# A 128-byte pad among the constants of a fused attention and two-layer feed-forward kernel

## The chip, the cores and the metric

The kernel runs on one core of one Trainium2 chip. A core has five engines that run side by side: TensorE (PE, with its weight loads shown as PEld), VectorE (DVE), ScalarE (ACT), GpSimd (POOL) and SyncE (SP, which only issues transfers here). They work on SBUF, which has 128 partitions, and on PSUM, where matmuls leave their sums. The metric is the device time of one execution in microseconds (us). Before the change the median of two runs is 689.15 us (688.72 and 689.59).

## The reference

Three stages follow each other. Everything is float32, and the weights of the two feed-forward layers come as float64.

```
kv  = einsum('bhsd,bhse->bhde', k, v)            # 4 x 8 heads, 576 tokens, 64 wide, no softmax
out = einsum('bhsd,bhde->bhse', q, kv)
out = out / sqrt(mean(out*out) + 1e-6) * g_norm  # per token and head
x   = out as [2304 tokens, 512]
x   = (x @ w_a) * (x @ w_b) @ w_out              # 512 -> 1536 -> 512
h   = x @ w_in                                   # 512 -> 1024
s   = h * softmax(h)
y   = (s - mean(s)) / sqrt(var(s) + 1e-6) * g_ln
return y @ moe2_w_out                            # 1024 -> 512
```

## The kernel before, in words

The kernel keeps float32 accuracy by splitting operands into a high and a low part in the format fp32r and adding three matmuls for each product (high by high, high by low, low by high; `three` at lines 763 to 767, and the loop at line 850).

**Attention** (lines 602 to 755). Per batch, `pkv` is k-transposed times v (L602, L609), copied to the block-diagonal tiles `bd` (L615). Per tile of 128 tokens, `o` is q times `bd` (L647); it is squared and summed, the root is taken on POOL (L677, with the constant `mhalf`), and the scaled tile is turned by a matmul against the constant `ident` (L742), then split into `xh` and `xl` (L754, L755). Later tiles are turned through DRAM instead.

**First layer**. Weights arrive as float64 bits (`raw`), and are decoded into high and low float32 parts by ACT, DVE and POOL (lines 333 to 354, 435 to 437), into the ring of tiles `wh`/`wl`. `ab` (L765 to L767) takes `wh`/`wl` as the stationary operand and `xh`/`xl` as the moving one; `y` (L850) takes `wh`/`wl` as stationary and `gh`/`gl` as moving, and DVE adds its result to `ya` (L863).

**Second layer**. `h` (L1013) is made with a scheme of seven products of half-size blocks, from `late` tiles (left) and `wd` or `late` tiles (left); `out` (L765 to L767 by way of `run_o`) takes `dh` (right) or a piece of a `late` tile (left) as stationary and `wh_o`/`wl_o` (right) or a piece of a `late` tile (left) as moving.

**What sets the order.** A planner, `Order`, runs while the program is written: it keeps a clock and a table of costs for each engine, and decides from them which matmul group, vector operation or transfer is written next. Its costs know nothing of addresses. On the chip every engine then runs its own list in that order, and semaphores hold it back where data is missing. All transfers are issued by SP.

**Where buffers lie.** SBUF is given out from both ends. The pools `cst` (constants), `xs` (`xh`, `xl`, later the `late` tiles), `att` (`bd`, `kv`, `tail`, `q`, `qs`, `x`, `sq`, `r`) and, in the place of `att`, `w2` (`wd`, `bt`) are opened with side="left". The pools `wp` (`wh`, `wl`), `yp` (`ya`), `ph1` (`raw`, `u`, `f`, `a`, `gh`, `gl`) and, in the place of `ph1`, `ph2` (`st`, `u`, `ot`, `dh`) with side="right". The change stands among the first lines that take tiles, 192 to 201:

```
    ident = cst.tile([P, P], F32, tag="ident", name="ident")
    ...
    mhalf = cst.tile([P, H], F32, tag="mhalf", name="mhalf")

    nc.gpsimd.memset(mhalf, -0.5)
    ...
    make_identity(nc, ident)
```

Of the kernel before, what the change touches and what calls it, by code (L numbers as in the profile page):

```python
# [9 lines left out]
F32 = mybir.dt.float32  # L10
# [7 lines left out]
P = 128  # L18
# [128 lines left out]
def attention_moe_moe_kernel(ctx: ExitStack, tc, kv_in, kv_tail, q_in, g_norm, w1, w_in, w_out2, g_ln, out):  # L147
# [3 lines left out]
    nc = tc.nc  # L151
    INF = float("inf")

    cst = ctx.enter_context(tc.tile_pool(name="cst", bufs=1, side="left"))
# [38 lines left out]
    gn = cst.tile([P, 1], F32, tag="gn", name="gn")  # L193
    gl_sb = cst.tile([P, NF2], F32, tag="gln", name="gln")
    mhalf = cst.tile([P, H], F32, tag="mhalf", name="mhalf")

    nc.gpsimd.memset(mhalf, -0.5)
    bds = [att.tile([P, NP, P], F32, tag=f"bd{n}", name=f"bd{n}", bufs=1) for n in range(2)]
# [1192 lines left out]
```

## Time and profile before

| | |
|---|---|
| median of two runs | 689.15 us (688.72 to 689.59) |
| the profiled execution | 688.91 us |
| its span, first to last instruction | 687.1 us |
| PE busy | 672.2 us (98%) |
| DVE, ACT, POOL busy | 522.9, 277.0, 274.6 us |
| granted TensorE clock, mean | 0.999 |

The profile is of one execution. Its span is 1.8 us shorter than that execution's time, and 2.05 us shorter than the median of the runs. A PE that is 98% busy says that some matmul was under way nearly always; how closely matmuls follow each other is read from their start times. Buffer numbers are left out of names, so `wh_w` stands for every high part of a first-layer weight.

### The profile page before, as it was taken

The page shows a single profiled execution, that of the slowest core. Times are in us where ns is not written, and L with a number is a line of the kernel's source. Part 1 is how long each engine was busy: PE and PEld are TensorE (multiplying, and loading weights), DVE is VectorE, ACT ScalarE, POOL GpSimd, SP SyncE. Part 2 cuts the span into 40 slices and gives each one's busy share as a digit, 9 for nine tenths or more (in the row PEclk, how much of TensorE's full clock was granted, in tenths as well). Part 3 has the DMA queues.
Part 4 walks back from the last instruction along what each step waited for, and adds up shares of the span by engine and source line. Part 5 has one row for each costly group of instructions (what it writes and reads, how often), then busy time and mean ns, then how long its engine had stood idle before and what let it go on. Part 6 is the DMA issues. An engine that isn't in the chain of part 4 may idle for free.

```text
span 687.1 us, 9551 instructions
## 1 busy us (share of the span) xinstructions
PE 672.2 (98%) x3530; PEld 582.8 (85%) x3530; DVE 522.9 (76%) x754; ACT 277.0 (40%) x481; POOL 274.6 (40%) x276
## 2 busy tenths in 40 slices
PE   5899999999999999999999999999999999999998
PEld 4799888989888898989898988889778888888887
DVE  2988875689989899889789798555559878766850
ACT  3768244423332333332233232211257665653531
POOL 1848213244374534633332232301448656651100
PEclk9999999999999999999999999999999999999999
DMA  8974340123242221123141422013422654354451
GB/s 328 374 269 134 106 139 1 62 96 119 92 154 93 79 74 62 62 93 124 61 154 65 133 80 93 0 62 114 174 80 83 193 155 129 103 151 139 152 170 47
DMA packets 63694, 82.42 MB, mean 120 GB/s; under 512 B 6176, under 2 KB 45344, under 8 KB 63648
## 3 DMA queue, kind: packets, MB, share of 16 engines
q1 hardware_dynamic: 63648, 81.81, 36.2%
q8 instruction: 28, 0.46, 0.3%
q14 instruction: 18, 0.15, 0.1%
HBM read 59.25 MB, written 22.54 MB: 119 GB/s over the span
## 4 chain that ended last, share of the span: by engine, by line
PE 93%; DMA 3%; SPq 1%; ACT 1%; DVE 1%; POOL 1%; issue 0%; ACTq 0%
PE y L850 21%; PE ab L765 14%; PE ab L767 14%; PE ab L766 14%; PE h L1013 13%; PE out L766 5%; PE out L767 5%; PE out L765 5%; PE o L647 1%; DMA kv<-in_kv 1%; DMA raw_w<-in_w 1%; DMA q<-in_q 1%; POOL r L677 1%; SPq L276 1%; PE pkv L602 0%; PE t L742 0%
## 5 line engine op out<-in xcount | busy, mean ns | idle before, releaser
L765 PE MATMUL ab<-xh,wh_w 128*128 128x512 f32 (+1 forms) x480 | 178.1, 371 | 0.0
L766 PE MATMUL ab<-xl,wh_w 128*128 128x512 f32 (+1 forms) x480 | 176.9, 369 | 0.2 <-DVE xl L755 0.2
L767 PE MATMUL ab<-xh,wl_w 128*128 128x512 f32 (+1 forms) x480 | 177.0, 369 | 0.0
L863 DVE TENSOR_TENSOR ya<-y,ya 128x1024 f32<-128x1024 f32 (+1 forms) x110 | 122.3, 1111 | 4.1 <-PE y L850 3.9
L819 ACT COPY a<-ab 128x512 f32<-128x512 f32 (+1 forms) x60 | 32.6, 544 | 204.5 <-PE ab L767 204.4
L436 POOL TENSOR_TENSOR f_w<-f_w,wh_w 128x512 f32<-128x512 f32 x36 | 48.3, 1343 | 157.1 <-ACT wh_w L435 87.2
L765 PEld LDWEIGHTS ab<-xh,wh_w 128*128 128x128 f32 x480 | 90.2, 188 | 12.9 <-DVE ya L863 1.0
L766 PEld LDWEIGHTS ab<-xl,wh_w 128*128 128x128 f32 x480 | 90.2, 188 | 12.0 <-DVE xl L755 0.5
L767 PEld LDWEIGHTS ab<-xh,wl_w 128*128 128x128 f32 x480 | 90.1, 188 | 11.3
L820 DVE TENSOR_TENSOR ab<-ab,a 128x512 f32<-128x512 f32 (+1 forms) x60 | 38.7, 644 | 72.1 <-ACT a L819 72.0
L850 PE MATMUL y<-gl,wh_w 128*128 128x512 f32 (+1 forms) x240 | 88.5, 369 | 0.3 <-DVE gl L822 0.3
L850 PE MATMUL y<-gh,wl_w 128*128 128x512 f32 (+1 forms) x240 | 88.5, 369 | 0.0
L850 PE MATMUL y<-gh,wh_w 128*128 128x512 f32 (+1 forms) x240 | 88.4, 368 | 0.0
L1013 PE MATMUL h<-wd,lateh 128*128 128x512 f32 x216 | 58.5, 390 | 0.7 <-ACT bt L1050 0.7
L943 POOL TENSOR_TENSOR lateh<-ya,lateh 128x512 fp32r<-128x512 f32 (+1 forms) x18 | 21.1, 1189 | 74.0 <-ACT lateh L942 74.0
L850 PEld LDWEIGHTS y<-gl,wh_w 128*128 128x128 f32 x240 | 45.0, 188 | 6.6 <-DVE gl L822 0.8
L437 POOL TENSOR_TENSOR wl_w<-f_w,u_w 128x512 fp32r<-128x512 f32 x36 | 47.7, 1328 | 6.0 <-DVE u_w L354 4.3
L850 PEld LDWEIGHTS y<-gh,wh_w 128*128 128x128 f32 x240 | 45.1, 188 | 5.8
L850 PEld LDWEIGHTS y<-gh,wl_w 128*128 128x128 f32 x240 | 45.1, 188 | 5.6
L1013 PEld LDWEIGHTS h<-wd,lateh 128*128 128x128 f32 x216 | 40.4, 188 | 9.5 <-ACT bt L1050 1.2
L821 ACT CAST gh<-ab 128x512 fp32r<-128x512 f32 (+1 forms) x60 | 32.7, 545 | 33.7 <-DVE ab L820 32.5
L1013 PE MATMUL h<-latel,lateh 128*128 128x512 f32 x162 | 45.7, 390 | 0.0
(114 smaller groups left out, 1164.6 us busy)
## 6 DMA issues: line engine op xcount, KB each, us to landing
raw_w<-in_w SPq DMA_DIRECT2D x36, 512.0 KB, 3.3
su<-ya SPq DMA_DIRECT2D x34, 256.0 KB, 2.9
ya<-su SPq DMA_DIRECT2D x34, 256.0 KB, 3.0
kv<-in_kv SPq DMA_DIRECT2D x16, 512.0 KB, 7.5
out<-ot SPq DMA_DIRECT2D x17, 256.0 KB, 3.2
raw_i<-in_w_in SPq DMA_DIRECT2D x8, 512.0 KB, 3.4
raw_o<-in_w_out SPq DMA_DIRECT2D x8, 512.0 KB, 3.7
so<-raw_o SPq DMA_DIRECT2D x8, 512.0 KB, 2.7
```

The lines of the kernel that those rows point to most:

```text
L436: ("T", 1.32, lambda: nc.gpsimd.tensor_tensor(out=f, in0=f, in1=hi.bitcast(F32), op=ALU.subtract)),
L437: ("T", 1.38, lambda: nc.gpsimd.tensor_tensor(out=lo, in0=f, in1=u, op=ALU.add)),
L765: nc.tensor.matmul(o, lhsT=ah, rhs=bh, start=first, stop=False)
L766: nc.tensor.matmul(o, lhsT=ah, rhs=bl, start=False, stop=False)
L767: nc.tensor.matmul(o, lhsT=al, rhs=bh, start=False, stop=last)
L819: ("A", 0.45 * k, lambda: nc.scalar.copy(out=a, in_=ps[:, 0, 0:nb])),
L820: ("V", 0.54 * k, lambda: nc.vector.tensor_tensor(out=g, in0=g, in1=a, op=ALU.mult)),
L821: ("A", 0.45 * k, lambda: nc.scalar.copy(out=gh, in_=g)),
L850: nc.tensor.matmul(o, lhsT=x[:, s], rhs=y, start=f == fs[0] and n == 0, stop=f == fs[-1] and n == 2)
L863: op = ("V", 0.9 * nb / NB, lambda: nc.vector.tensor_tensor(out=dst, in0=src, in1=dst, op=ALU.add))
L943: ("G", 2.15 * cost, lambda: nc.gpsimd.tensor_tensor(out=lo[:, n], in0=src, in1=hi[:, n].bitcast(F32), op=ALU.subtract)),
L1013: nc.tensor.matmul(o, lhsT=x, rhs=y, start=first and k == m == 0, stop=k == 1 and m == 2, skip_group_check=not first)
```

## The change

Two lines are added after the constants. They take a tile `pad` of 32 float32 per partition, 128 bytes, and have POOL fill it with zeros. No instruction reads it.

```
     mhalf = cst.tile([P, H], F32, tag="mhalf", name="mhalf")
+    pad = cst.tile([P, 32], F32, tag="pad", name="pad")
+    nc.gpsimd.memset(pad, 0.0)
 
     nc.gpsimd.memset(mhalf, -0.5)
```

The addresses that the two built programs give to tiles, in bytes from the start of a partition:

| tile (side) | before | after |
|---|---|---|
| `ident`, `gn`, `gln`, `mhalf` (left, constants) | 16512, 17024, 17056, 17088 | the same |
| `pad` (left) | none | 17120 |
| `xh0`, later `lateh0` (left) | 17120 | 17248 |
| `xl0`, later `latel0` (left) | 37600 | 37728 |
| `bd0`, later the first `wd` (left) | 90848 | 90976 |
| first `kv`, later the second `wd` (left) | 94944 | 95072 |
| `bt` (left) | 123616 | 123744 |
| the four `r` (left) | 135904, 135936, 135968, 136000 | each 128 more |
| first `raw` (right) | 137184 | the same |
| eight `st` (right) | 138464, then every 96 bytes | the same |
| `gh` (right) | 159712 and 161760 | the same |
| `ya0` (right) | 167904 | the same |
| first `wh` (right) | 204768 | the same |

So 103 tiles move up by 128 bytes, which are all on the left side but the four constants that are taken ahead of the pad. The two sides still don't touch: the left side ends at 136160 now, and the right side begins at 137184. Each main tile of both sides begins 224 bytes above a multiple of 256 before the change; after it those of the left side begin 96 bytes above one.

On POOL the first instructions of the kernel's own part are these before the change (`const` tiles are set by the launch code ahead of them):

```order
L197 MEMSET mhalf 128x8
masks.py:197 MEMSET ident 128x128
masks.py:199 ISA
masks.py:199 AFFINE_SELECT ident<-ident 128x128
L436 TENSOR_TENSOR f_w_0_123<-f_w_0_123,wh_w_0_199 128x512
```

And these after it, where line numbers below the change are two higher:

```order
L197 MEMSET pad 128x32
L199 MEMSET mhalf 128x8
masks.py:197 MEMSET ident 128x128
masks.py:199 ISA
masks.py:199 AFFINE_SELECT ident<-ident 128x128
L438 TENSOR_TENSOR f_w_0_125<-f_w_0_125,wh_w_0_201 128x512
```

One memset stands ahead of `mhalf`; from there on POOL's list is the old one, and the lists of the other engines hold the same instructions in the same order. POOL counts one instruction more, so the numbers that others wait for on its semaphore are one higher.

## Rows read from the trace of the kernel before

**Rows 1.** The page: busy us (share of the span) xinstructions, by engine.

```profile
PE 672.2 (98%) x3530; PEld 582.8 (85%) x3530; DVE 522.9 (76%) x754; ACT 277.0 (40%) x481; POOL 274.6 (40%) x276
```

**Rows 2.** Chain that ended last: shares of the span by engine.

```profile
PE 93%; DMA 3%; SPq 1%; ACT 1%; DVE 1%; POOL 1%; issue 0%; ACTq 0%
```

**Rows 3.** Waits of PE: who waited for whom, us in total, times, longest.

```profile
PE pkv L602 <- DMA kv<-in_kv: 7.6, 4, 4.1
PE t L742 <- DVE r L672: 0.8, 1, 0.8
PE o L647 <- DMA q<-in_q: 0.7, 1, 0.7
...
PE ab L766 <- DVE xl L755: 0.2, 1, 0.2
```

**Rows 4.** Timeline, POOL and DVE, first 15 us: start us, us, engine, line, operation.

```profile
0.72 0.10 POOL L197 MEMSET mhalf<- 128x8 f32 x1 [0.29 <-POOLq L1381]
...
0.76 0.20 POOL masks.py:197 MEMSET ident<- 128x128 f32 x1
0.90 1.03 DVE L200 MEMSET bd<- 128x512 f32 x2 [0.90 <-PEq L1381]
1.04 0.29 POOL masks.py:199 TENSOR_SCALAR_AFFINE_SELECT ident<-ident 128x128 f32<-128x128 f32 x1
...
12.74 1.26 POOL L436 TENSOR_TENSOR f_w<-f_w,wh_w 128x512 f32<-128x512 f32 x1 [11.41 <-ACT wh_w L435]
```

**Rows 5.** By line: xcount: duration ns min/median/max, first and last start us.

```profile
L647 PE MATMUL o<-bd,q x128: 270/275/580, 13.6 to 85.5; 128*128 128x128 f32 x128
...
L742 PE MATMUL t<-ident,x x48: 270/272/328, 21.3 to 66.4; 128*128 128x128 f32 x48
...
L677 POOL TENSOR_TENSOR r<-r,mhalf x18: 1630/1734/2397, 18.4 to 88.7; 128x8 f32<-128x8 f32 x18
...
L1086 POOL TENSOR_TENSOR st<-st x18: 192/193/196, 517.0 to 653.7; 128x1 f32<-128x1 f32 x18
L1087 POOL TENSOR_SCALAR st<-st x18: 264/265/267, 517.3 to 657.2; 128x1 f32<-128x1 f32 x18
```

**Rows 6.** PE by line and shape: xcount, busy us, mean ns.

```profile
L766 PE MATMUL ab<-xl,wh_w 128*128 128x512 f32 x288 | 112.5, 391 | 0.0
...
L1013 PE MATMUL h<-wd,lateh 128*128 128x512 f32 x216 | 58.5, 390 | 0.7 <-ACT bt L1050 0.7
...
L850 PE MATMUL y<-gl,wh_w 128*128 128x512 f32 x144 | 56.3, 391 | 0.3 <-DVE gl L822 0.3
...
L765 PE MATMUL out<-latel,dh 128*128 128x512 f32 x34 | 13.2, 389 | 0.0
```

**Rows 7.** Timeline of PE from 199.74 us: twelve y between ab of 384 columns.

```profile
199.74 0.33 PE L766 MATMUL ab<-xl,wh_w 128*128 128x384 f32 x1
...
201.13 0.39 PE L850 MATMUL y<-gh,wh_w 128*128 128x512 f32 x1
...
203.89 0.33 PE L765 MATMUL ab<-xh,wh_w 128*128 128x384 f32 x1
...
204.41 0.35 PE L765 MATMUL ab<-xh,wh_w 128*128 128x384 f32 x1
204.60 0.34 PE L766 MATMUL ab<-xl,wh_w 128*128 128x384 f32 x1
```

**Rows 8.** By stretch: PE, PEld, DVE, ACT, POOL busy us (x), clock, DMA share, GB/s.

```profile
0.00:20.00 20.00, 12.43 (x142) 11.22 (x144) 7.48 (x17) 8.55 (x20) 4.89 (x10) 1.00 0.92 336
...
100.00:300.00 200.00, 200.00 (x964) 175.93 (x963) 171.51 (x241) 67.89 (x119) 92.58 (x68) 1.00 0.24 81
```

**Rows 9.** DMA issues: KB each, median us to landing.

```profile
kv<-in_kv SPq DMA_DIRECT2D x16, 512.0 KB, 7.5
...
si<-wd SPq DMA_DIRECT2D x6, 512.0 KB, 2.7
```

## The prediction

> **What bounds the kernel now.** I read the shares of the engines first, then the chain of waits, then what PE waits for, then the times at which matmuls start. PE is busy 672.2 of 687.1 us [rows 1] and makes up 93% of the chain that ended last [rows 2]. That leaves 687.1 - 672.2 = 14.9 us in which PE has no matmul under way. Eight waits, from 7.6 us down to 0.2 us, add up to 11.4 us of it, and the largest is the four times that it waits for `kv` to land [rows 3]; the rest, 3.5 us, lies behind the last matmul. So no wait that is given back can bring more than 11.4 us, which is 1.7% of 688.9.
>
> A busy share doesn't tell whether the matmuls run at their full pace, so I read their starts. Twelve y matmuls of 512 columns start between 201.13 and 203.89 us, 2.76 / 12 = 0.230 us apart; eight matmuls of 384 columns start between 199.74 and 201.13, 1.39 / 8 = 0.174 us apart [rows 7]. The granted clock is 1.00 in both stretches listed, which is the level of 2.4 GHz [rows 8]; 512 columns at one per cycle would be 0.213 us, 384 would be 0.160. Matmuls follow each other with about 0.015 us over that, and little stands between them. The kernel is a stream of matmuls with DVE as the next busiest: in the stretch from 100 to 300 us DVE works 171.51 of 200 us [rows 8], so its operations would have to become 200 / 171.51 = 1.17 times as long before they could set the pace there.
>
> **The change part by part.**
>
> *The added memset.* POOL fills 128 x 32 elements. The nearest rows are the fill of 128 x 8 with 0.10 us and that of 128 x 128 with 0.20 us [rows 4]; I take 0.10 us, since 32 is nearer to 8, with ends of 0 (POOL's fills start 0.04 us apart though each lasts longer, so it may overlap) and 1.03 us, the length of the two DVE fills beside which it would run, should it have to wait until they are through. It stands ahead of `mhalf`, `ident` and the select on POOL's queue. Of what is queued behind it, `mhalf` is first used by the root at L677, from 18.4 us; `ident` by the transpose at L742, from 21.3 us [rows 5]; POOL's own next work starts at 12.74 us after 11.41 us of idle time [rows 4]. The select is through at 1.04 + 0.29 = 1.33 us; with 1.03 us more it would be 2.36. So POOL's idle 11.41 us hide even the upper end: term 0. The pad adds no transfer; no queue of SP, ACT, DVE or PE gets an instruction, and the count that POOL's waits look for is one higher because POOL also counts one more.
>
> *The move of 103 tiles by 128 bytes, for matmuls.* This is the term that the whole forecast hangs on, since PE is the bound. `ab` streams a left tile past weights from the right, `y` has both operands on the right, `h` both on the left, and one form of `out` streams a left tile past a right one. Their means for 512 columns are 391, 391, 390 and 389 ns [rows 6]. So the pace doesn't depend on whether the two operands lie on the same side or on two. There is a hole in this evidence: all main tiles of both sides begin 224 bytes above a multiple of 256, so their distance was a whole number of 256 bytes, and a pair of sides that stand 128 bytes out of step is new. The nearest row with another distance is the transpose, whose `ident` begins 128 and whose `x` begins 224 above a multiple of 256, 96 bytes out of step: its median is 272 ns, against 275 ns for the attention product `bd` by `q`, which are in step [rows 5]. Being out of step costs nothing there, so I take 0. The ends come with the two rivals on matmuls, below.
>
> *The move, for DVE, ACT and POOL.* The eight `st` tiles begin at 96-byte distances, so they stand at eight places between multiples of 256; the eighteen POOL operations on them at L1086 take 192 to 196 ns [rows 5]. A start address that moves by multiples of 32 bytes shows no effect there, and an effect would have to reach 17% on DVE to be felt (above). Term 0. As bounds from below and above I take the waits of PE for DVE in the rows, 0.8 us at most for one: 0.8 us less if they vanished, 0.8 more if they doubled.
>
> *The move, for transfers.* Loads into the left side are `kv`, `tail`, `q`, `qs`, and late ones. What they are worth is the wait for `kv`, 7.6 us in all [rows 3], in a stretch with a DMA share of 0.92 and 336 GB/s [rows 8], which is as dense as it gets. No row shows the same transfer at two start addresses. So the ends are minus 7.6 us (no wait left) and plus 7.6 us (the wait doubles); I take 0, since number, size and order of the transfers are unchanged and the new start is no rounder than the old. One rule of the Trainium skill names a boundary whose phase this change moves: DMA: Bandwidth & Descriptors, section How a descriptor splits into AXI transactions, says that a read which doesn't start on a multiple of 256 bytes fetches from the boundary below. By it the six stores of `wd` would read from 96 instead of 224 bytes above a boundary, 131 instead of 135 beats of 32 bytes per row of 4096 bytes, an estimate from that page; at 2.7 us each [rows 9] that is 6 x 2.7 x 4 / 135 = 0.5 us of transfer time that PE doesn't wait for, so by it the sum is the same. No run here shows the rule so far.
>
> *Sum.* 688.91 + 0 + 0 + 0 + 0 = 688.9 us for the profiled execution, which is 0.24 us under the median of the runs shown; against that median the forecast is **689.1 us**.
>
> **The rivals.**
>
> *Slower: operands out of step.* If the array's two operand streams, weights from the right and moving data from the left, get in each other's way when they stand 128 bytes out of step, each of the 3 x 480 `ab` matmuls pays. The nearest price is the slowest step between neighbours in the rows, 204.41 to 204.60 us, 0.19 us for 384 columns, against the usual 0.174 [rows 7]: 0.016 us x 1440 = 23 us, 712 us. It decides (2% of 688.9 is 13.8 us) from 13.8 / 1440 = 0.0096 us per matmul. For it: `ab` alone is 1440 of PE's 3530 matmuls [rows 1], and the distance is new. Against it: the transposes [rows 5].
>
> *Faster: in step was the bad case.* The 0.0167 us that a y matmul takes over 0.213 us could be the price of two streams in step, and the change would end it for `ab`: 0.0167 x 1440 = 24 us, 665 us. Against it: `y`, `h` and `out` pay the same though their distances differ by many different multiples, and most of those pairs lie on one side and would keep it.
>
> *Another start.* The first loads land earlier or later, or the roots at L677, which take 1.63 to 2.40 us [rows 5], fall differently against DVE. By the ends of the transfer term that gives 681.3 to 696.5 us: on either side of the forecast, and within 2% of it.
>
> *The pad does nothing.* If the tiles had not moved, the time would be that of before, 689.1 us too. The addresses speak against it: `xh0` begins at 17248 instead of 17120. It changes no number here.
>
> **How the numbers follow.** No change by more than a few us: 0.91. Another start with several us on either side: 0.04. Operands out of step: 0.03. In step was the bad case: 0.01. What is left, 0.01, is for a slowdown that I don't see. 2%, which is 675 to 703 us, is about what a measurement of this kernel can tell from no change. Faster by over 2%: 0.01, from the second rival alone, since all waits together are 11.4 us. Slower by over 2%: 0.04, from the first and the unseen. Within 2%: 0.95. The two runs of before lie 0.9 us apart; for another program I allow some 2 us below and 3 above, more above since PE has nearly no idle time to give back: 687.0 to 692.0. The two rivals on matmuls, most of the other starts and part of the first case's own tails are left out with that, together less than 2 in 10.
>
> **What would show it.** The `pad` fill at about 0.7 us on POOL with some 0.1 us, and POOL idle for some 11 us after the select. Means of 389 to 391 ns for all forms of 512 columns, and starts 0.230 us apart. PE's wait for `kv` near 7.6 us. What would prove it wrong: `ab` with another pace than `y`, or the longest of the waits for `kv` several us away from 4.1 us [rows 3] with the same list of transfers ahead of it; a span that differs while all of these stand as before would put the cause outside the argument.

## The result: 1% slower, and all of it in the pace of matmuls

The changed kernel takes 696.22 us (median of 695.82 and 696.61) against 689.15 us: a ratio of 1.0111, with an interval of 1.0094 to 1.0128. Its profiled execution has a span of 694.0 us, 6.9 us more than before.

The engines' busy times on the page of the changed kernel, to be held against [rows 1]:

```profile
PE 679.0 (98%) x3530; PEld 583.5 (84%) x3530; DVE 523.3 (75%) x754; ACT 277.5 (40%) x481; POOL 274.3 (40%) x277
```

PE is busy 6.8 us longer with the same 3530 matmuls; DVE, ACT, POOL and the weight loads moved by less than 1 us. So the loss is inside the time in which matmuls are under way, not in waits. The waits of PE confirm it; the longest of them after the change, against [rows 3]:

```profile
PE pkv L604 <- DMA kv<-in_kv: 7.5, 3, 4.1
PE t L744 <- DVE r L674: 1.0, 1, 1.0
PE t L744 <- DVE xl L757: 0.8, 1, 0.8
```

The matmuls of 512 columns by line and operands after the change (count, busy us, mean ns), against [rows 6]; line numbers are two higher than before:

```profile
L767 PE MATMUL ab<-xh,wh_w 128*128 128x512 f32 x288 | 114.1, 396 | 0.0
L769 PE MATMUL ab<-xh,wl_w 128*128 128x512 f32 x288 | 113.7, 395 | 0.0
L768 PE MATMUL ab<-xl,wh_w 128*128 128x512 f32 x288 | 113.7, 395 | 0.0
L1015 PE MATMUL h<-wd,lateh 128*128 128x512 f32 x216 | 58.6, 391 | 0.7 <-ACT bt L1052 0.7
L852 PE MATMUL y<-gl,wh_w 128*128 128x512 f32 x144 | 56.4, 391 | 0.3 <-DVE gl L824 0.3
...
L768 PE MATMUL out<-wl_o,dh 128*128 128x512 f32 x102 | 40.4, 396 | 0.0
...
L769 PE MATMUL out<-wh_o,lateh 128*128 128x512 f32 x54 | 21.4, 397 | 0.0
...
L767 PE MATMUL out<-latel,dh 128*128 128x512 f32 x34 | 13.4, 394 | 0.0
L768 PE MATMUL out<-latel,dh 128*128 128x512 f32 x34 | 13.3, 390 | 0.0
```

`h`, with both operands on the left, and `y`, with both on the right, stand where they stood (391 against 390, 391 against 391). `ab`, with one operand on each side, went from 391 to 395 or 396, and forms of `out` that have an operand on each side, or whose next matmul has, from 389 to between 394 and 397. One form is an exception: `out<-latel,dh` of L768 has an operand on each side and stays at 390. The starts tell the same more sharply, since durations are modelled. Two stretches of `ab` of 512 columns, first and last row of each; before the change:

```profile
415.37 0.39 PE L766 MATMUL ab<-xl,wh_w 128*128 128x512 f32 x1
...
417.18 0.39 PE L850 MATMUL y<-gh,wh_w 128*128 128x512 f32 x1
```

and after it, with the load of the next weights beside one of them:

```profile
419.53 0.39 PE L769 MATMUL ab<-xh,wl_w 128*128 128x512 f32 x1
...
420.00 0.39 PE L768 MATMUL ab<-xl,wh_w 128*128 128x512 f32 x1
420.00 0.19 PEld L769 LDWEIGHTS ab<-xh,wl_w 128*128 128x128 f32 x1
...
421.16 0.39 PE L852 MATMUL y<-gh,wh_w 128*128 128x512 f32 x1
```

Before, 8 steps take 1.81 us, 0.226 each; after, 7 steps take 1.63 us, 0.233 each. Nothing waits in either. Single stretches scatter (the `y` of [rows 7] start 0.230 us apart, in step), so the whole trace decides: over the 859 steps under 0.26 us from an `ab` of 512 columns the mean went from 0.2278 to 0.2331 us. Summed over the start times of all matmuls in both traces, `ab` lost 5.4 us (4.6 us in the forms of 512 columns, 0.8 in those of 384), `out` 1.9 us, `h` and `y` together 0.2 us, and the attention part gained 0.5: 7.0 us up to the start of the last matmul, where the span's end came 6.9 us later than before. The delay grows steadily from about 85 us to the end.

### The profile page after: what moved, and what is told of

Its sections match the earlier page's. It is cut to its first block, busy times and chain, and to the rows that moved or that the text cites. A ratio compares the mean times of both kernels' runs of the same rounds, so it can differ in the third digit from the quotient of the medians.

```text
span 694.0 us, 9552 instructions
## 1 busy us (share of the span) xinstructions
PE 679.0 (98%) x3530; PEld 583.5 (84%) x3530; DVE 523.3 (75%) x754; ACT 277.5 (40%) x481; POOL 274.3 (40%) x277
## 4 chain that ended last, share of the span: by engine, by line
PE 94%; DMA 3%; DVE 1%; POOL 1%; ACT 1%; issue 0%; SPq 0%; ACTq 0%
PE y L852 21%; PE ab L767 15%; PE ab L768 14%; PE ab L769 14%; PE h L1015 12%; PE out L769 5%; PE out L768 5%; PE out L767 5%; PE o L649 1%; DMA raw_w<-in_w 1%; DMA kv<-in_kv 1%; DMA q<-in_q 1%; POOL r L679 1%; PE t L744 1%; DVE xl L757 0%; PE pkv L604 0%
## 5 line engine op out<-in xcount | busy, mean ns | idle before, releaser
L767 PE MATMUL ab<-xh,wh_w 128*128 128x512 f32 (+1 forms) x480 | 180.5, 376 | 0.0
L768 PE MATMUL ab<-xl,wh_w 128*128 128x512 f32 (+1 forms) x480 | 178.4, 372 | 0.3 <-DVE xl L757 0.3
L768 PEld LDWEIGHTS ab<-xl,wh_w 128*128 128x128 f32 x480 | 90.2, 188 | 13.4 <-DVE xl L757 0.6
```

The costliest lines, as they stand in the source:

```text
L767: nc.tensor.matmul(o, lhsT=ah, rhs=bh, start=first, stop=False)
L768: nc.tensor.matmul(o, lhsT=ah, rhs=bl, start=False, stop=False)
```

## The experiments

Each run is compared with runs of the kernel before on the same chip, whose medians were 688.85 us (the first four runs below), 688.29 (the next four) and 688.88 (the last four). "In step" below means that the start addresses of two operands differ by a whole number of 256 bytes.

Theory S: matmuls pay when their two operands are out of step. Rival I: the extra POOL instruction, or the counts on its semaphore, cost the time. Rival A: the place of the left tiles alone counts.

**A pad of 256 bytes.**

```
+    pad = cst.tile([P, 64], F32, tag="pad", name="pad")
+    nc.gpsimd.memset(pad, 0.0)
```

> A pad of 256 bytes with its fill in the place of the pad of 128: the extra POOL instruction stays, and the left side moves up by a whole multiple of 256 bytes, so that left and right tiles begin in step modulo 256 again. Theory S (matmuls pay when their operands come from two sides that are out of step modulo some power of two up to 256 bytes): 689 us, ab of 512 columns back to a mean of 391 ns. Theory I (the extra instruction on POOL, or the counts that it shifts, costs the 7 us): 696 us. Theory A (what counts is where the left tiles begin against 256 bytes, whatever the right side does): 689 us.

Measured: 688.36 us, ratio 0.9997 (0.9986 to 1.0007). The extra instruction is there and costs nothing, so rival I is out. In its trace `ab` is back:

```profile
L767 PE MATMUL ab<-xh,wh_w 128*128 128x512 f32 x288 | 112.6, 391 | 0.2
```

**128 bytes on both sides.**

```
+    rpad = ctx.enter_context(tc.tile_pool(name="rpad", bufs=1, side="right"))
     wp = ctx.enter_context(...)
...
+    pad = cst.tile([P, 32], F32, tag="pad", name="pad")
+    nc.gpsimd.memset(pad, 0.0)
+    pad_r = rpad.tile([P, 32], F32, tag="pad_r", name="pad_r")
+    nc.gpsimd.memset(pad_r, 0.0)
```

> The pad of 128 bytes on the left and another of 128 bytes at the outer end of the right side, both filled by POOL: every main tile of both sides begins 96 bytes above a multiple of 256, and the two sides are in step again. Theory S (distance between the sides): 689 us, all forms of 512 columns at 389 to 391 ns. Theory A (place of the left tiles alone): 696 us, or more if tiles of the right side pay too. Theory I (extra instructions): 696 us or more, since there are two.

Measured: 688.54 us, ratio 0.9995 (0.9983 to 1.0007). The left tiles lie exactly where the slow kernel has them, and the time is that of before: rival A is out, as is I once more. `ab` is back here too:

```profile
L770 PE MATMUL ab<-xh,wh_w 128*128 128x512 f32 x288 | 112.5, 391 | 0.0
```

**128 bytes on the right side alone.**

```
+    rpad = ctx.enter_context(tc.tile_pool(name="rpad", bufs=1, side="right"))
...
+    pad_r = rpad.tile([P, 32], F32, tag="pad_r", name="pad_r")
+    nc.gpsimd.memset(pad_r, 0.0)
```

> The pad of 128 bytes on the right side alone; every left tile begins where it began in the kernel before. Theory S (distance between the sides, now 128 bytes out of step with the opposite sign): 696 us, with ab at a mean of some 396 ns and y and h as before. Theory A (place of the left tiles): 689 us. Theory I (one extra POOL instruction): 696 us, but with the loss spread over other lines than ab and out.

Measured: 695.44 us, ratio 1.0091 (1.0072 to 1.0110). The loss comes back with no left tile moved, in the same lines:

```profile
L768 PE MATMUL ab<-xh,wh_w 128*128 128x512 f32 x288 | 114.1, 396 | 0.0
...
L853 PE MATMUL y<-gl,wh_w 128*128 128x512 f32 x144 | 56.4, 391 | 0.3 <-DVE gl L825 0.3
```

**The left side up by 64 bytes, with no instruction added.**

```
-    mhalf = cst.tile([P, H], F32, tag="mhalf", name="mhalf")
+    mhalf = cst.tile([P, H + 16], F32, tag="mhalf", name="mhalf")
```

> No pad and no extra instruction: the constant mhalf is 24 instead of 8 wide (all of it filled by the same one instruction), which moves the left side up by 64 bytes. Theory S with a period of 256 bytes: slower than 689 us, between it and 696 if the cost grows with the distance up to 128 bytes, about 696 if any distance costs the same. Theory S with a period of 128 bytes can't be, since 128 bytes cost 7 us. Theory I: 689 us. Theory A: not 689, no size follows from it.

Measured: 691.70 us, ratio 1.0038 (1.0024 to 1.0051). It is slower with the old list of instructions, so a loss needs no extra instruction, and it is smaller than at 128 bytes.

**A gap of 128 bytes between the weight ring and the rest of the right side.**

```
+    gap = ctx.enter_context(tc.tile_pool(name="gap", bufs=1, side="right"))
     yp = tc.alloc_tile_pool(name="yp", bufs=1, side="right")
...
+    pad_g = gap.tile([P, 32], F32, tag="pad_g", name="pad_g")
+    nc.gpsimd.memset(pad_g, 0.0)
```

> A pad of 128 bytes on the right side between the weight ring (wh, wl, which stays) and all that lies below it (ya, gh, gl, raw, dh, which move by 128). Now ab has its left operand in step with wh and wl, while y has two operands on the same side that are out of step, and out has dh out of step with wh_o. Theory S1 (what counts is the distance between the two operands that TensorE reads, wherever they lie): ab back to 391 and 336 ns and starts 227 ns apart, y slower by the 5.5 ns per matmul of 512 columns and 1.4 ns of 384 that ab lost, 432 x 5.5 + 288 x 1.4 = 2.8 us, and out slower by 1 to 2 us: 692.5 to 694 us. Theory S2 (it is the two ends of SBUF that matter, left against right): y unchanged, ab unchanged, 689 to 690 us.

Measured: 692.98 us, ratio 1.0065 (1.0048 to 1.0082), inside the range of S1. The loss changes lines:

```profile
L768 PE MATMUL ab<-xh,wh_w 128*128 128x512 f32 x288 | 112.7, 391 | 0.0
L769 PE MATMUL ab<-xl,wh_w 128*128 128x512 f32 x288 | 112.3, 390 | 0.0
...
L853 PE MATMUL y<-gh,wl_w 128*128 128x512 f32 x144 | 56.9, 395 | 0.0
L853 PE MATMUL y<-gl,wh_w 128*128 128x512 f32 x144 | 56.9, 395 | 0.3 <-DVE gl L825 0.3
L853 PE MATMUL y<-gh,wh_w 128*128 128x512 f32 x144 | 56.8, 395 | 0.0
```

`ab`, across the two sides but in step, is at 390 and 391; `y`, on one side but out of step, is at 395. So what counts here is the distance of the operands and not the side on which they lie.

**Other distances.** The left side up by 32, 96, 192, 160 and 224 bytes, each by the width of `mhalf` as above (`H + 8`, `H + 24`, `H + 48`, `H + 40`, `H + 56`).

> mhalf 16 instead of 8 wide, one fill as before, so that the left side moves up by 32 bytes. 128 bytes cost 6.6 us and 64 bytes 2.7. If the cost grows with the distance from a multiple of 256: some 1.3 us, 690 us. If any distance that isn't a multiple of 64 is bad in itself: 692 us or more. If being in step is not the best place but only one of the good ones: under 688 us.

> mhalf 32 instead of 8 wide, left side up by 96 bytes. If the cost grows with the distance from a multiple of 256: between 2.7 and 6.6 us, some 693 to 694 us. If multiples of 64 have a cost of their own: apart from that line in either direction.

> mhalf 56 instead of 8 wide, left side up by 192 bytes, which is 64 bytes short of a multiple of 256. If only the distance to the nearest multiple counts: as with 64 bytes, 691.7 us. If the direction counts (the moving operand ahead of or behind the weights): another time, up to 696 us or down to 689.

> mhalf 48 wide, left side up by 160 bytes, the mirror of 96. 32, 64, 96, 128, 192 bytes gave 697, 692, 699, 695, 696 us, so odd multiples of 32 were the worst: 696 to 699 us, with ab slower and y and h as before.

> mhalf 64 wide, left side up by 224 bytes, the mirror of 32. As for 160 bytes: 696 to 699 us if odd multiples of 32 are the worst. Under 689 us if this one distance is a better place than in step, which would make it the kernel to keep.

**16 bytes, for `ab` alone.**

```
-        xh[hf] = xs.tile([P, NP, n], F32R, tag=f"xh{hf}", name=f"xh{hf}")
+        xh[hf] = xs.tile([P, NP * n + 64], F32R, tag=f"xh{hf}", name=f"xh{hf}")
+        xh[hf] = xh[hf][:, 4:4 + NP * n].rearrange("p (c t) -> p c t", c=NP)
...
```

(the same for `xl`, and the `late` tiles, which take their place, are 64 elements longer and used from their start)

> The four tiles of xh and xl are 64 elements longer, which keeps all else on the left in step, and ab streams them from 16 bytes further up, so that ab alone is out of step by 16 bytes; late tiles, bd, kv, wd and bt are in step. If the cost hangs on pieces of 32 bytes or more: 689 us. If 16 bytes are enough to be out of step: slower, up to the 697 of 32 bytes less what out costs there, some 695. If there is a better place than in step between the multiples of 32: under 688 us.

Measured, with the kernels above:

| left against right, bytes past a multiple of 256 | us | ratio (interval) |
|---|---|---|
| 0 (pad of 256) | 688.36 | 0.9997 (0.9986 to 1.0007) |
| 16 (`ab` alone) | 693.04 | 1.0059 (1.0042 to 1.0075) |
| 32 | 696.94 | 1.0121 (1.0105 to 1.0138) |
| 64 | 691.70 | 1.0038 (1.0024 to 1.0051) |
| 96 | 698.75 | 1.0144 (1.0127 to 1.0161) |
| 128 (the change) | 696.22 | 1.0111 (1.0094 to 1.0128) |
| 160 | 696.00 | 1.0107 (1.0090 to 1.0125) |
| 192 | 696.37 | 1.0116 (1.0100 to 1.0132) |
| 224 | 695.08 | 1.0095 (1.0080 to 1.0110) |

Every distance tried costs something, down to 16 bytes, and none is better than in step. My expectation that the cost grows with the distance fell: 32 bytes cost three times what 64 cost. At 64 bytes one form of `ab` that is out of step like the others, `ab<-xh,wl`, didn't slow at all (390 ns, where `ab<-xh,wh` took 394). 64 and 192 differ, so which of the two operands lies ahead counts as well, or the place of the left tiles by itself: the two were held apart only in step and at 128 bytes, by the runs with pads on both sides and on the right alone. In the same way the 16-byte run moves the start of the streamed tiles off a multiple of 32 bytes, and no run tells that from the distance. Of the two last ones, which I had put at 696 to 699 us, 224 bytes came out 0.9 us below.

**128 bytes between high and low weights.** In `take_wc`, at the first call, a tile is put between the two halves of the ring:

```
+        if wc_slot[k] == 0:
+            hi = wp.tile([P, CH], F32R, tag="wh", name=...)
+            nc.gpsimd.memset(wp.tile([P, 32], F32, tag="wpad", name="wpad", bufs=1), 0.0)
+            return hi, wp.tile([P, CH], F32R, tag="wl", name=...)
```

> 128 bytes between the high and the low weights in the ring: wl stays, wh and all that lies below it on the right (ya, gh, gl, raw, dh) move by 128. So in ab the operands wh and x are out of step and wl and x in step; in y wh and g are in step and wl and g out of step. ab runs (wh,xh), (wh,xl), (wl,xh); y runs (wh,gh), (wh,gl), (wl,gh). Theory N (a matmul is slowed by the load of the next one's weights, if those are out of step with what it streams): ab<-xh,wh and ab<-xh,wl at 396 and 395 ns, ab<-xl,wh at 391; y<-gl,wh slower than before by 5 ns, y<-gh,wl and y<-gh,wh as before. Theory O (a matmul is slowed by its own weights if they are out of step with what it streams): ab<-xh,wh and ab<-xl,wh slow, ab<-xh,wl at 391; y<-gh,wl slow and the other two as before. If both count: all of ab slow, and two of the three forms of y. Time 692 to 696 us under either.

Measured: 697.21 us, ratio 1.0122 (1.0107 to 1.0137), over the range I gave.

```profile
L771 PE MATMUL ab<-xh,wl_w 128*128 128x512 f32 x288 | 114.0, 396 | 0.0
L769 PE MATMUL ab<-xh,wh_w 128*128 128x512 f32 x288 | 114.0, 396 | 0.0
L770 PE MATMUL ab<-xl,wh_w 128*128 128x512 f32 x288 | 113.6, 394 | 0.0
...
L854 PE MATMUL y<-gh,wl_w 128*128 128x512 f32 x144 | 57.1, 396 | 0.0
L854 PE MATMUL y<-gl,wh_w 128*128 128x512 f32 x144 | 57.0, 396 | 0.3 <-DVE gl L826 0.3
L854 PE MATMUL y<-gh,wh_w 128*128 128x512 f32 x144 | 56.5, 392 | 0.0
```

`ab<-xl,wh` has its own weights out of step and the next ones in step: 394. `ab<-xh,wl` has its own in step and the next ones out: 396. `y<-gh,wl` (own) and `y<-gl,wh` (next) are both at 396, and `y<-gh,wh`, which has neither, is at 392. So neither N nor O alone holds: on average a matmul slows if its own weights or the next ones are out of step with what it streams. The starts of all fourteen traces say the same: by the addresses of the built programs, matmuls of 512 columns start 0.2279 us apart on average if both weights are in step, 0.2323 if only their own are 128 bytes out, 0.2333 if only the next ones are, and 0.2330 if both are, so the two don't add up. Single forms depart from it: `out<-latel,dh` of L768 in the changed kernel has its own weights 128 bytes out and keeps 0.2275.

## Why the prediction was wrong, step by step

- **What bounds the kernel** was right: the loss is PE's, and the idle time outside its stream stayed the same (687.1 - 672.2 = 14.9 us before, 694.0 - 679.0 = 15.0 after). Of the 3.5 us that the prediction puts behind the last matmul, some 3.2 lie there; the rest is in small gaps.
- **The memset** was right. It took 0.13 us, and all behind it on POOL had time to spare. POOL's first rows after the change, against [rows 4]:

```profile
0.72 0.13 POOL L197 MEMSET pad<- 128x32 f32 x1 [0.29 <-POOLq L1383]
0.78 0.10 POOL L199 MEMSET mhalf<- 128x8 f32 x1
...
1.10 0.29 POOL masks.py:199 TENSOR_SCALAR_AFFINE_SELECT ident<-ident 128x128 f32<-128x128 f32 x1
...
13.26 1.27 POOL L438 TENSOR_TENSOR f_w<-f_w,wh_w 128x512 f32<-128x512 f32 x1 [11.86 <-ACT wh_w L437]
```

- **The terms for DVE, ACT, POOL and transfers** were right at 0: busy times within 0.6 us of before, the wait for `kv` 7.5 against 7.6 us, and the stores of `wd` landing after 2.7 us in both. The stretch of 336 GB/s isn't "as dense as it gets", since the page of before has a slice with 374 GB/s; nothing hangs on that.
- **The term for matmuls, taken as 0, is the step that failed.** The prediction named the hole, that all pairs of main tiles were in step, and filled it with the transposes, of which it said that being out of step costs nothing there. The runs showed a cost in its place: 5.3 ns for each `ab` of 512 columns, 5.4 us in all of `ab` and 1.9 us in `out`. The prediction's own sign of being wrong, `ab` with another pace than `y`, is what came. The transposes were the wrong rows to read it from. They are of 128 columns and another format (float32, where the others are fp32r), and neither their distance of 224 bytes after the change, nor the 0 bytes that they have in the run with the left side up by 160, changed their pace:

```profile
L744 PE MATMUL t<-ident,x x48: 270/272/328, 21.8 to 66.1; 128*128 128x128 f32 x48
```

and in that run:

```profile
L742 PE MATMUL t<-ident,x x48: 270/272/332, 21.8 to 65.4; 128*128 128x128 f32 x48
```

  An operation that takes the same time in step and out of step can't stand for one that does not.
- **The rival "operands out of step"** had the mechanism, with a chance of 0.03 and a price that was too high. Its step of 0.016 us came from two neighbours that were in step, so it had another cause. `ab` paid 5.4 / 1440 = 0.0038 us per matmul on average, under the point of 0.0096 from which it would have passed 2%; the price named was 23 us for `ab`, and 5.4 was measured. It also left out `out`, where another 1.9 us are.
- **The rival "in step was the bad case"** is refuted: no distance tried is faster.
- **The rival "another start"** reaches up to 696.5 us, and the measured 696.22 lies inside, but that is chance: its cause, a longer wait for first loads, didn't come (7.5 us for `kv`).
- **The range** had been left without the rival's smaller prices. A mechanism whose price is known only from a far row should have been priced from 0 up to that row, not at that row alone; the chance of something between 692 and 703 us was set too low by that. Nor is 2% what can be told from no change, as the prediction has it: eight runs of the 64-byte kernel tell 0.4% from it (1.0024 to 1.0051).

What is shown: what costs the time is how the start addresses of the fp32r matmuls' operands lie to each other modulo 256 bytes, since the runs with a wider `mhalf` lose time with the list of instructions unchanged; a shift of 256 bytes or of both sides costs nothing, and the loss moves to the lines whose operands are put out of step. It isn't shown that the distance sets the time of every single matmul, and some in step slow down beside others that are out of step. In the run with the left side up by 160 bytes this form, with both operands and the next weights on the right, went from 389 to 397 ns; before the change, and in that run:

```profile
L765 PE MATMUL out<-wh_o,dh 128*128 128x512 f32 x102 | 39.7, 389 | 0.0
...
L765 PE MATMUL out<-wh_o,dh 128*128 128x512 f32 x102 | 40.5, 397 | 0.0
```

What is only argued: that the stream of the moving operand and a load of weights meet in SBUF. A weight load starts at the very time at which the matmul before it starts (420.00 us above), so it can meet that matmul's stream, which fits the cost of next weights out of step. It doesn't explain the cost of a matmul's own weights, whose load is over (420.00 + 0.19 us) before that matmul starts (420.23). The Trainium skill, SBUF — State Buffer, section Who interferes with whom, calls TensorE's read ports for the two operands independent. In these runs the pace hangs on both operands' addresses together; whether that comes about at these ports isn't shown. It also stays open why the cost isn't even over the distances, why 384 columns pay 1.3 ns where 512 pay 5.3, and why in the 16- and 32-byte runs one form of `y`, in step itself, also went from 389 to 393 ns (`y<-gh,wh`).

## What to carry to other kernels

In a kernel like this one, which TensorE bounds with fp32r matmuls that each load new weights, keep the start addresses of the moving and the stationary operand, and of the stationary operand of the next matmul, a whole multiple of 256 bytes apart; a small tile among the constants shifts everything behind it. Sizes of pads and constants that are multiples of 256 bytes keep that up: the pad of 256 costs nothing here, that of 128 costs 1.1%. Other formats weren't looked at, but for the float32 transposes of 128 columns, which didn't react. When a change only moves buffers, compare matmul start steps line by line, since busy shares (98% in both kernels) and waits show nothing of it.

## What the runs showed of the hardware that I had not expected

- After an `ab` matmul of 512 columns in fp32r the next one starts 0.2278 us later on average when in step, and 0.2331 when 128 bytes out of step, at the same granted clock of 0.999.
- 16 bytes out of step, for `ab` alone, are enough to cost 0.6% of the kernel; of the distances tried, 96 bytes cost the most, 1.4%.
- Vector, scalar and GpSimd operations and transfers showed nothing of the shift by 128 bytes: DVE busy 522.9 us before and 523.3 after, POOL 274.6 and 274.3.
